# An attention-and-expert kernel on one core: a new order of all its operations, with some sixty of them on another engine

## The chip, the cores and the metric

The kernel runs on one core of a Trainium2 chip. The metric is device time in microseconds of one execution. The core has a matmul engine (TensorE, PE in the profile, with its weight loads as PEld), three engines for elementwise work (VectorE or DVE, ScalarE or ACT, GpSimd or POOL) and a queue for transfers between the chip's memory and the core (SyncE or SP). Each engine takes its instructions strictly in the order in which the program lists them; engines wait for each other through semaphores.

## The reference

A recurrent attention over 768 steps for 4 batches and 8 heads of size 48, then a feed-forward block in which the larger of two projections goes on:

```python
state = np.zeros((B, H, D, D))
for t in range(S):
    kt, vt, rt, wt = k[:, :, t], v[:, :, t], r[:, :, t], w[:, :, t]
    cur = np.einsum('bhd,bhe->bhde', u[None] * kt, vt)
    y[:, :, t] = np.einsum('bhd,bhde->bhe', rt, state + cur)
    state = wt[:, :, :, None] * state + np.einsum('bhd,bhe->bhde', kt, vt)
x = y.transpose(0, 2, 1, 3).reshape(B * S, H * D)      # 3072 x 384
out = np.maximum(x @ w1, x @ w2) @ w_out               # d_ff = 1024
```

All inputs and the output are float32.

## The kernel before

The recurrence is computed in chunks. A unit is one chunk of 256 steps of one or two batches; `UNITS` names eight: units 0 to 3 have one batch each and the first chunk, units 4 and 5 the second chunk and units 6 and 7 the third, with two batches each. For each unit the kernel loads w, k, r and v; takes logarithms of products of w and sums them over time on PE (`wp`, `ln`, `hi`, `lo`, `ex`); makes the sums' exponentials (`mz`, `ie`, `e0`); multiplies r and k by them (`rw`, `kw`, `scale`); transposes the results into the tile RK, on PE with an eviction (`tr`, `te`, units 0 to 4) or by DMA (`dt`, units 5 to 7); forms scores (`sc`), puts the masked ones into the tile M (`mk`), whose diagonal with u comes from `rk`, `ru`, `dg`, `dd` and `di`; computes the state (`kv`, `st`, `sm`, `sb`) and the output of the attention (`ya`, `yi`), which `xe` moves to xT. `vb` casts v to bf16.

The maximum is taken as max(a, b) = b + max(a - b, 0). So `wdiff` forms w1 - w2 in three pieces of 128 rows, `gt` multiplies xT by it, `rl` is the eviction with max(., 0), and `op` adds xT times the product w2 w_out (`wc`, made once by `w2turn`, `w2take`, `wocast`, `wfold`) and the rl result times w_out. `oe` evicts and `os` stores. `hot` are matmuls whose result nobody reads; 48 of them fill PE at fixed places in the order, eight or sixteen at a time.

A name like `scale.0.1.0.1@p` reads: the operation, the unit, its further arguments, and the engine (`@d` DVE, `@a` ACT, `@p` POOL); names without one have a fixed engine. For `scale` the arguments are 0 for r or 1 for k, the batch, and the half of the heads (units of two halves: unit 0 only). For `dt` they are r or k, and the batch.

What sets the order is one table, `ORDER`, of 652 such names. The program walks it once and issues each operation in that sequence, so it fixes the order on every engine and in the DMA queue, and the engine of each operation that may run on several. There is no scheduler beside it. On GpSimd operations of two full halves are issued as two pieces (`by_two`); on VectorE as one. Buffers are limited: four PSUM banks G for `ex`, `tr`, `w2turn`, `gt`, `op` and `hot`, two pairs Y for `sc`, `kv` and the attention's output. DMAs take eight semaphores in turn, so each is issued only when the one eight places before it has landed.

```python
for o in ORDER:
    o, _, e = o.partition("@")
    name, *a = o.split(".")
    a = [int(x) if x.isdigit() else x for x in a] + ([e] if e else [])
    if name in ops:
        ops[name](*a)
    else:
        unit[name](U[a[0]], *a[1:])
```

In the profile most elementwise products stand under line 176 (`mul`, one piece) or 180 (two pieces) and most copies and evictions under line 168 (`copy`), since helpers record them: the tile's name tells them apart. The other lines: 234 `hot`, 398 `ex` (395 and 396 from unit 3 on), 440 `mz`, 502 `dg`, 516 `di`, 565 `tr`, 596 `kv`, 615 `st`, 641 `sc`, 650 `mk`, 675 `yi`, 688 `ya`, 706 `gt`, 717 and 719 `rl`, 725 and 729 `op`, 743 `os`.

Of the kernel before, what the change touches and what calls it, by code (L numbers as in the profile page):

```python
# [53 lines left out]
zero.k.1@p zero.M.1@p load.1.w.0 zero.m@p mask zero.k.0@d load.0.w.0 u ident identb@p identq@a tri
wp.0.0@p ln.0.0 zero.s.0@d hot.8.3 zero.o@p load.0.k wp.1.0@d load.0.w.1 load.0.r wp.0.1@d hot.8.0
kw.0.1@p ln.0.1 ex.0.1 load.1.k ex.0.0 ln.1.0 wload.1.1 kw.0.0@p mz.0.0 ie.0.0 zero.v.1@d wt.0.0
uspread mz.0.1 ie.0.1 e0.0.1 zero.v.0@d wt.0.1 rw.0.1@d rk.0.0@d scale.0.0.0.1@d utake@a hot.8.2
we.0.0 load.1.r hot.8.1 rw.0.0@p ru.0.0@d zero.r@d e0.0.0 scale.0.0.0.0@d we.0.1 scale.0.1.0.1@p
scale.0.1.0.0@p ex.1.0 load.2.w.0 tr.0.0.0 zero.s.1@p te.0.0.0@a tr.0.0.1 te.0.0.1@a w2turn.1.0
load.0.v vb.0.0@a vb.0.1@p dg.0 load.1.v rk.1.0@d dd.0@a ru.1.0@d mz.1.0 sc.0.0.0.0 wload.1.2 kv.0  # L60
dg.1 ie.1.0 w2take.1.0@a sc.0.0.1.0 kw.1.0@p w2turn.2.0 load.3.w.0 wp.2.0@d vb.1.0@a st.0.0@a ln.2.0
di.0.0@d zero.M.0@p st.0.1 rw.1.0@d load.2.r wt.1.0 mk.0.0.0.0 sm.0@p w2take.2.0@a sc.0.0.1.1
sc.0.0.0.1 mk.0.0.0.1 mk.0.0.1.1 ex.2.0 we.1.0 e0.1.0 hot.8.5 vb.1.1@a dd.1@a zero.v.2@d sb.0.0@a
mz.2.0 scale.1.1.0.0@p scale.1.0.0.0@d ie.2.0 load.2.k rk.2.0@d w2turn.2.1 w2take.2.1@a tr.1.0.1
# [6 lines left out]
ru.2.0@d xe.1.0@a rl.0.2@a row.2 sm.1@d gt.1.1 load.3.r load.3.k rk.3.0@d gt.1.3 woload.2 mz.3.0
wocast.0@a rl.0.1@a ie.3.0 sc.2.0.1.0 woload.1 dg.2 dd.2@a rl.1.3@d kv.2 rl.1.1@d gt.0.3 st.2.0@a
rl.0.3@a woload.3 gt.1.0 st.2.1 gt.1.2 zero.M.2@p di.2.0@d e0.3.0 rw.3.0@p wocast.2@p load.3.v
sc.2.0.0.0 scale.3.0.0.0@d kw.3.0@p mk.2.0.0.0 gt.0.0 mk.2.0.1.0 ru.3.0@d wocast.1@p wocast.3@a
sb.2.0@a wfold.1 load.4.w.0 wp.4.0@d rl.1.0@a wfold.0 rl.1.2@a vb.3.1@d dg.3 wctake.0@a sb.2.1@a
scale.3.1.0.0@p wfold.2 ln.4.0 hi.4@d wctake.2@a dd.3@d ya.2.0.1.0 wctake.1@a di.3.0@d lo.4@d
rl.0.0@a row.3 ya.2.0.0.0 load.4.k load.4.r rk.4.0@d vb.3.0@p yi.2.0 kv.3 st.3.0@a st.3.1 xe.2.0@a
tr.3.0.0 te.3.0.0@a op.1.1 rk.4.1@d oe.1.1@a tr.3.0.1 te.3.0.1@a gt.2.0 gt.2.2 rl.2.2@a rw.4.0@d
gt.2.1 ru.4.1@p load.4.v wl.2 load.5.w.0 rl.2.1@a ex.4.0 mz.4.0 ex.4.1 wl.3 mz.4.1 row.4 rl.2.0@a
e0.4.1 sc.3.0.0.0 mk.3.0.0.0 sc.3.0.1.0 ie.4.0 gt.2.3 rl.2.3@a vb.4.1@a op.0.0 oe.0.0@a os.1.1  # L80
e0.4.0 sb.3.1@a vb.4.0@a op.0.1 sb.3.0@a scale.4.0.1.0@d oe.0.1@a mk.3.0.1.0 kw.4.0@p ru.4.0@d
ya.3.0.0.0 scale.4.1.1.0@d ya.3.0.1.0 scale.4.1.0.0@d yi.3.0 we.3 scale.4.0.0.0@d xe.3.0@a tr.4.1.1
tr.4.1.0 dg.4 sm.3@p load.5.k op.1.0 wp.5.0@p load.5.r te.4.1.0@a te.4.1.1@a ln.5.0 gt.3.2 oe.1.0@d
gt.3.0 sc.4.1.1.0 kv.4 hi.5@a tr.4.0.0 rl.3.0@a rl.3.2@a dd.4@d di.4.1@d tr.4.0.1 di.4.0@d lo.5@d
mk.4.1.1.0 gt.3.1 st.4.0 we.2 te.4.0.0@a sm.2@p st.4.1 rk.5.1@d load.6.w.0 op.2.1 te.4.0.1@a
rl.3.1@a rk.5.0@p ru.5.0@d oe.2.1@a sc.4.1.0.0 mk.4.1.0.0 sb.4.1@a load.5.v sc.4.0.1.0 gt.3.3
mk.4.0.1.0 ex.5.1 kw.5.0@p load.6.r ex.5.0 rl.3.3@a sb.4.0@a op.2.0 oe.2.0@a ya.4.1.0.0 ya.4.1.1.0
os.2.0 mz.5.0 mz.5.1 wl.4 rw.5.0@p row.5 sc.4.0.0.0 ru.5.1@p load.6.k op.3.0 e0.5.0 vb.5.1@a
mk.4.0.0.0 e0.5.1 ie.5.0 yi.4.1 xe.4.1@a oe.3.0@a scale.5.0.1.0@d yi.4.0 ya.4.0.1.0 ya.4.0.0.0
xe.4.0@a scale.5.0.0.0@d dt.5.0.0 op.3.1 wp.6.0@p ln.6.0 gt.4.6 dg.5 dd.5@a scale.5.1.0.0@d dt.5.1.0  # L90
rl.4.6@a gt.4.7 rl.4.7@a gt.4.0 we.4 rl.4.0@a gt.4.2 hi.6@d dt.5.0.1 gt.4.1 di.5.1@d oe.3.1@a
rl.4.2@a gt.4.4 vb.5.0@a scale.5.1.1.0@d sm.4@d lo.6@d gt.4.5 rk.6.1@d rl.4.4@a gt.4.3 rl.4.3@a
ex.6.0 rk.6.0@d kw.6.0@p rl.4.1@a kv.5 ru.6.0@p sc.5.0.1.0 di.5.0@d st.5.0 mk.5.0.1.0 st.5.1
rw.6.0@p rl.4.5@a op.4.2 ex.6.1 mz.6.1 sc.5.0.0.0 e0.6.1 dt.5.1.1 sc.5.1.0.0 os.1.0 mk.5.0.0.0
sb.5.0@a mk.5.1.0.0 op.4.3 load.7.w.0 mz.6.0 oe.4.3@a load.6.v e0.6.0 ya.5.0.0.0 ru.6.1@p oe.4.2@a
ya.5.0.1.0 ie.6.0 sc.5.1.1.0 mk.5.1.1.0 os.4.3 os.0.1 op.4.0 ya.5.1.0.0 sb.5.1@a ya.5.1.1.0 yi.5.1
load.7.k oe.4.0@a yi.5.0 op.4.1 dg.6 xe.5.1@a scale.6.0.1.0@d oe.4.1@a xe.5.0@d scale.6.0.0.0@d
dt.6.0.1 gt.5.1 wp.7.0@p scale.6.1.0.0@d ln.7.0 gt.5.3 rl.5.3@d gt.5.4 rl.5.4@a dd.6@d gt.5.6
vb.6.0@a gt.5.0 rl.5.0@a di.6.1@d rl.5.1@a hi.7@d di.6.0@d rl.5.6@a lo.7@d scale.6.1.1.0@p gt.5.7
rl.5.7@a vb.6.1@p kv.6 gt.5.2 rl.5.2@a load.7.r rk.7.0@d gt.5.5 ru.7.0@p dt.6.1.1 ex.7.1 mz.7.1  # L100
rl.5.5@a op.5.1 sc.6.1.0.0 rk.7.1@p dt.6.1.0 st.6.0 mk.6.1.0.0 ru.7.1@p dt.6.0.0 os.4.2 sc.6.1.1.0
mk.6.1.1.0 op.5.2 sb.6.0@a oe.5.2@a ex.7.0 mz.7.0 sc.6.0.1.0 wl.5 we.5 kw.7.0@p mk.6.0.1.0 os.3.1
sc.6.0.0.0 mk.6.0.0.0 op.5.3 os.3.0 ya.6.1.0.0 sb.6.1@a e0.7.1 rw.7.0@d ya.6.1.1.0 ie.7.0 os.4.1
e0.7.0 oe.5.3@a ya.6.0.1.0 scale.7.0.1.0@d ya.6.0.0.0 yi.6.0 yi.6.1 xe.6.0@a scale.7.0.0.0@d
oe.5.1@d op.5.0 xe.6.1@a gt.6.6 rl.6.6@a oe.5.0@a gt.6.2 load.7.v vb.7.0@a os.5.1 gt.6.5 rl.6.5@a
vb.7.1@a scale.7.1.0.0@p dt.7.1.0 gt.6.4 scale.7.1.1.0@p dg.7 dd.7@a dt.7.0.0 dt.7.0.1 rl.6.4@d
# [691 lines left out]
```

## Time and profile before

| | us |
|---|---|
| three runs | 151.09, 152.08, 153.25 |
| median of the runs | 152.08 |
| the profiled execution's own time | 149.86 |
| its span, first to last instruction | 148.2 |
| its mean granted TensorE clock | 0.977 of full |

Times in the tables that follow are microseconds from the start of the span. The profile's groups give the operation's busy time, the mean of one, and the idle time of the engine just before it with what ended it. A row of the timeline has the start, the length, the engine, the line, the operation with what it writes and reads, and how often; in brackets the idle time before it. An engine that idles costs nothing by itself: what counts is whether the work that the end waits for is held up.

### The profile page before, as it was taken

The numbers are of one execution on the slowest core, as the hardware profiler recorded it, in microseconds if no ns is written. First come the engines' busy times: TensorE is split into PE (matmuls) and PEld (weight loads), VectorE is DVE, ScalarE is ACT, GpSimd is POOL, SyncE is SP. The second block draws the span as 40 slices with busy tenths as digits, with TensorE's granted clock in tenths as the row PEclk, the third lists the DMA queues.
The fourth block names the chain that finished last, engine by engine and source line by source line (L and its number), as shares of the span: only waits on it lengthen the run. The fifth ranks groups of instructions, "written<-read, shape, count | busy, mean of one in ns | idle before, by whom it ended". The sixth has DMA issues, their size and how long they took to land.

```text
span 148.2 us, 5523 instructions
## 1 busy us (share of the span) xinstructions
PE 137.9 (93%) x2404; PEld 85.0 (57%) x2404; DVE 115.0 (78%) x160; ACT 93.7 (63%) x173; POOL 76.4 (52%) x94
## 2 busy tenths in 40 slices
...
GB/s 110 297 357 302 338 269 374 372 247 269 250 234 287 237 123 87 316 286 215 223 68 245 179 170 272 286 233 282 186 250 131 90 172 241 110 214 5 0 164 106
DMA packets 71188, 31.85 MB, mean 215 GB/s; under 512 B 66294, under 2 KB 70391, under 8 KB 71163
## 3 DMA queue, kind: packets, MB, share of 16 engines
...
q8 instruction: 19, 0.31, 0.9%
...
## 4 chain that ended last, share of the span: by engine, by line
PE 62%; DVE 13%; ACT 7%; DMA 5%; POOL 4%; issue 4%; SPq 2%; POOLq 1%; DVEq 0%; ACTq 0%
PE G L706 15%; PE G L729 15%; PE G L234 7%; PE G L725 6%; DVE M L650 5%; PE Y L688 4%; PE Y L641 3%; DMA lw<-in_w_dram 3%; PE G L318 3%; ACT RK L168 3%; DMA RK<-rp 2%; PE Y L675 2%; PE G L398 2%; POOL kp L180 2%; PE Y L596 1%
## 5 line engine op out<-in xcount | busy, mean ns | idle before, releaser
L729 PE MATMUL G<-wo_sb,gT 128*128 128x384 bf16 x192 | 35.1, 326 | 0.0
L706 PE MATMUL G<-xT,wd_sb 128*128 128x256 bf16 (+1 forms) x192 | 33.9, 326 | 0.1
L650 DVE CAST_PREDICATED M<-mask,Y 128x1024 bf16<-128x1024 int32 (+1 forms) x26 | 28.7, 1133 | 3.0 <-PE Y L641 2.9
L717 ACT ACTIVATE gT<-G 128x512 bf16<-128x512 f32 x41 | 23.4, 599 | 6.2 <-PE G L706 5.9
L729 PEld LDWEIGHTS <-gT 128*128 128x128 bf16 x192 | 18.8, 98 | 12.4
L706 PEld LDWEIGHTS <-wd_sb 128*128 128x128 bf16 x192 | 18.1, 98 | 12.5 <-issue 0.5
L180 POOL TENSOR_TENSOR rku<-rku,u_b 128x384 f32<-128x384 f32 x12 | 12.5, 1065 | 13.1 <-DVE rku L176 13.1
L234 PE MATMUL G<-S_b 128*128 128x512 bf16 x48 | 15.4, 488 | 2.1 <-DVE S_b L263 2.1
L725 PE MATMUL G<-wc_sb,xT 128*128 128x384 bf16 x72 | 15.7, 328 | 0.0
L168 ACT COPY RK<-G 128x1024 bf16<-128x1024 bf16 x12 | 11.8, 1016 | 6.0 <-PE G L565 6.0
L168 ACT COPY osb<-G 128x384 f32<-128x384 f32 x13 | 6.2, 477 | 12.7 <-PE G L729 10.8
L180 POOL TENSOR_TENSOR kp<-lk,iE 128x384 bf16<-128x384 f32 x10 | 11.2, 1147 | 1.8 <-issue 1.8
L234 PEld LDWEIGHTS <-S_b 128*128 128x128 bf16 x48 | 5.6, 123 | 11.0 <-issue 6.6
L168 ACT CAST xT<-Y 128x768 bf16<-128x768 f32 x10 | 10.2, 1033 | 2.4 <-PE Y L688 1.4
L502 DVE TENSOR_REDUCE dg<-rku 128x16 f32<-128x768 f32 x12 | 11.0, 944 | 0.0
L180 POOL TENSOR_TENSOR lk<-lk,lw 128x384 f32<-128x384 f32 x6 | 6.3, 1070 | 7.4 <-DVE rku L176 7.4
L641 PE MATMUL Y<-RK 48*64 48x128 bf16 x384 | 8.9, 220 | 1.2 <-ACT RK L168 0.5
L516 DVE TENSOR_TENSOR M<-identq,gd 128x512 int32<-128x512 int32 x12 | 9.0, 753 | 1.2 <-ACT gd L168 1.0
L440 DVE TENSOR_TENSOR MZ<-G,lg 128x384 f32<-128x384 f32 (+1 forms) x13 | 6.5, 513 | 3.6 <-PE G L398 2.1
L641 PEld LDWEIGHTS <-RK 48*64 48x64 bf16 x384 | 6.3, 106 | 4.9 <-issue 3.2
L688 PE MATMUL Y<-M,vp 64*32 64x128 bf16 x768 | 8.7, 219 | 0.3 <-DVE M L650 0.3
L176 DVE TENSOR_TENSOR rp<-lr,G 128x768 bf16<-128x768 f32 (+2 forms) x11 | 8.7, 795 | 0.4 <-ACT W L486 0.3
(108 smaller groups left out, 234.7 us busy)
## 6 DMA issues: line engine op xcount, KB each, us to landing
...
```

What stands on the lines that cost most here:

```text
L168: (nc.scalar.copy if e == "a" else nc.vector.tensor_copy if e == "d" else nc.gpsimd.tensor_copy)(o, i)
L180: op(o[:, g], a[:, g], b[:, g])
L234: nc.tensor.matmul(t, zz[:, 0:P], zz[:, 0:512], start=True, stop=True)
L502: nc.vector.reduce_sum(s.dg[:, b].rearrange("p i h -> p h i"), s.rku[:, b], axis=AX.X)
L516: (nc.vector if en == "d" else nc.gpsimd).tensor_tensor(out=o, in0=m, in1=g.unsqueeze(3).to_broadcast([P, 2, H, Q // 2]), op=ALU.bitwise_and)
L641: nc.tensor.matmul(t[q * Q:(q + 1) * Q, e, p * P:(p + 1) * P].rearrange("s (i g) -> s i g", i=2), s.kT[d, b, j, y * n + p, q, :], s.rT[d, ...
L650: nc.vector.copy_predicated(t[:, :, 2 * n * y:2 * n * (y + 1)].rearrange("s i (p e) g -> s p e i g", e=2), mask[:, j].bitcast(I32).unsquee ...
L688: nc.tensor.matmul(lhsT=s.vp[g, b, 2 * p + e, j, m * 32:(m + 1) * 32], rhs=s.M[b, j][g, :, 2 * p + e, :], **into(s, b, q, p * 96 + (e + m) ...
L706: nc.tensor.matmul(t[:, m * n * P:(m + 1) * n * P].rearrange("c (b t) -> c b t", t=P), wd_sb[:, ko, fo * P:(fo + 1) * P], s.xT[:, 0:n, ko, :],
L717: nc.scalar.activation(o, i, AF.Relu)
L725: nc.tensor.matmul(t[:, 0:HD], s.xT[:, a, ko, :], wc_sb[:, ko, :], start=(ko == 0), stop=False)
L729: nc.tensor.matmul(t[:, 0:HD], s.gT[:, c:c + P], wo_sb[:, f, :], start=False, stop=(f == FO - 1))
```

## The change

`ORDER` is written anew: the same 652 operations in another sequence, 66 of them on another engine. Nothing else in the program differs. Two lines of the table, as the diff has them, from the place where the differences of the weights stand:

```diff
-di.1.0@d mk.1.0.1.0 ln.3.0 wload.0.0 w2turn.0.1 w2take.0.1@a mk.1.0.0.0 trih@a vb.2.1@p ya.0.0.1.1
...
+woload.0 mk.1.0.1.0 wdiff.1@d tr.2.0.1 vb.2.0@a wdiff.0@d row.2 w2turn.1.0 load.3.r wdiff.2@d
```

Other engines: `wdiff.2`, `kw.0.0`, `rw.0.0`, `rw.3.0`, `wp.0.0`, `wp.5.0` to `wp.7.0`, `rk.5.0`, `ru.5.1`, `sm.3`, `sm.5` and `vb.3.0` go from GpSimd to VectorE; `rk.2.0`, `rk.5.1`, `rk.6.0`, `rk.7.0`, `kw.2.0`, `ru.3.0`, `ru.4.0`, `ru.5.0`, `scale.4.1.0.0`, `scale.5.1.0.0`, `scale.5.1.1.0` and `dd.3` from VectorE to GpSimd; `dd.0`, `dd.7`, `vb.1.0`, `vb.5.1` and `vb.6.0` from ScalarE to GpSimd, `wocast.1` the other way. Between VectorE and ScalarE casts of v, evictions (`oe`, `rl`, `xe`) and `hi` change in both directions, among them `vb.0.0`, `wocast.0`, `hi.3`, `rl.0.0` and `xe.3.0` to VectorE, `w2take.0.0`, `rl.1.1`, `hi.4` and `oe.1.0` to ScalarE.

On VectorE, around the forming of the weights' differences (the writes to wd_sb; M_81 is unit 1's scores, wb the turned w2, wst and lg the logarithms of unit 3). Before:

```order
L176 TENSOR_TENSOR rp_73<-lr,G 128x16x48
L615 TENSOR_TENSOR T<-Y,S_f 128x192
L516 TENSOR_TENSOR M_81<-identq,gd 128x2x256
L650 COPY_PREDICATED M_81<-mask,Y 128x8x2x64 x2
L168 CAST wb<-G 128x512
L176 TENSOR_TENSOR wd_sb<-gT 128x1024 x2
L413 SCALAR_TENSOR_TENSOR wst<-lg,wst 128x384
L176 TENSOR_TENSOR rku<-rku,u_b 128x768
```

Now:

```order
L176 TENSOR_TENSOR rp_73<-lr,G 128x16x48
L615 TENSOR_TENSOR T<-Y,S_f 128x192
L650 COPY_PREDICATED M_81<-mask,Y 128x8x2x64 x2
L176 TENSOR_TENSOR wd_sb<-gT 128x1024 x2
L176 TENSOR_TENSOR wd_sb<-wst 128x1024
L176 TENSOR_TENSOR rku<-rku,u_b 128x768
L168 CAST wo_sb<-wso 128x768
```

The third difference is now on VectorE, right behind the other two; the eviction to wb has left, and unit 1's diagonal (`di.1.0`) stands further up.

On GpSimd, in the head of the program, around the scaled keys of unit 0 (kp_74). Before:

```order
L176 TENSOR_TENSOR lw<-lk,lw 128x4x48 x2
L176 TENSOR_TENSOR lw<-lr,lw 128x4x48
L176 TENSOR_TENSOR kp_74<-lw,iE 128x4x48
L176 TENSOR_TENSOR kp_74<-lk,iE 128x4x48
L176 TENSOR_TENSOR kp_74<-lw,iE 128x4x48
L176 TENSOR_TENSOR kp_74<-lk,iE 128x4x48
L263 MEMSET S_b 128x1536
L168 CAST vp_76<-lv 128x4x2x48
L176 TENSOR_TENSOR lw<-lk,lw 128x8x48
```

Now:

```order
L186 AFFINE_SELECT mask<-mask 64x64 x2
L186 AFFINE_SELECT mask<-mask 64x128
L257 MEMSET M_81 128x1024
L176 TENSOR_TENSOR lw<-lk,lw 128x8x48
L176 TENSOR_TENSOR kp_74<-lw,iE 128x4x48
L176 TENSOR_TENSOR kp_74<-lk,iE 128x4x48
L176 TENSOR_TENSOR kp_74<-lw,iE 128x4x48
L176 TENSOR_TENSOR kp_74<-lk,iE 128x4x48
L168 CAST gd<-dg 128x32
L168 CAST vp_76<-lv 128x4x2x48
```

The mask, one clearing of M and the product for unit 1's keys (`kw.1.0`) now stand ahead of the scaled keys, the clearing of S_b stands at the program's start, and behind the keys comes the cast `dd.0` (gd).

In the DMA queue the loads of unit 0 now come first (half of w, r, k, u, the other half of w), then w of units 1 and 2; before, w of unit 1 came first. On PE the fillers at the start keep their sixteen matmuls; behind the first sums came sixteen more, and now eight come there and eight after unit 1's sums.

On GpSimd, where unit 5 is prepared (rku, lk, wso, kp_75; lg are the logarithms of later units, S_f the state). Before:

```order
L180 TENSOR_TENSOR rku<-wso,lk 128x384 x2
L180 TENSOR_TENSOR lk<-lk,wso 128x8x48 x2
L180 TENSOR_TENSOR wso<-wso 128x8x48 x2
L180 TENSOR_TENSOR rku<-rku,u_b 128x384 x2
L180 TENSOR_TENSOR lg<-lw 128x384 x2
L180 TENSOR_TENSOR lk<-lk,lw 128x8x48 x2
```

Now:

```order
L180 TENSOR_TENSOR rku<-rku,u_b 128x384 x2
L180 TENSOR_TENSOR rku<-wso,lk 128x384 x2
L180 TENSOR_TENSOR lk<-lk,wso 128x8x48 x2
L180 TENSOR_TENSOR wso<-wso 128x8x48 x2
L180 TENSOR_TENSOR kp_75<-lk,iE 128x8x48 x4
L168 CAST vp_76<-lv 128x8x2x48
```

Behind unit 5's four products now stand both its scaled keys (kp_75, four pieces) and a cast of v.

More of the change, by code (lines that the diff above doesn't have):

```diff
@@ L53 @@
 ORDER = """
[L54 to L64, printed above, removed]
@@ L71 @@
[L71 to L82, printed above, removed]
@@ L83 @@
[L83 to L106, printed above, removed]
@@ L113 @@
-oe.7.2@a op.7.0 os.7.2 oe.7.0@a os.6.1 os.7.0 op.7.3 oe.7.3@a os.7.3
+zero.o@p zero.s.0@d hot.8.1 load.0.w.0 ident hot.8.3 zero.s.1@p load.0.r wp.0.0@d ln.0.0 rw.0.0@d
+load.0.k u zero.r@d zero.M.2@p load.0.w.1 wp.0.1@d rw.0.1@d zero.v.0@d load.1.w.0 kw.0.0@d ln.0.1
+load.2.w.0 rk.0.0@d tri load.1.k ex.0.1 uspread utake@a ex.0.0 zero.m@p wp.1.0@d ln.1.0 identb@p
+mz.0.1 e0.0.1 ru.0.0@d wp.2.0@d mz.0.0 kw.0.1@p dg.0 mask zero.M.1@p hot.8.2 load.1.r rw.1.0@d
+kw.1.0@p wt.0.1 ex.1.0 ie.0.1 scale.0.1.0.1@p we.0.1 ie.0.0 scale.0.1.0.0@p dd.0@p zero.k.0@d wt.0.0
```

65 lines of the change are left out of this document (54 added, 11 removed).

## The prediction, made before the changed kernel had run

> **What bounds the kernel now.** I read the page's head first, then the table of busy time in three stretches of my own, then the timelines of the engines around the border of the first two. The head of the page:
>
> ```profile
> span 148.2 us, 5523 instructions
> PE 137.9 (93%) x2404; PEld 85.0 (57%) x2404; DVE 115.0 (78%) x160; ACT 93.7 (63%) x173; POOL 76.4 (52%) x94
> ```
>
> TensorE (PE) is busy in 93% of the span. Where the missing 10.3 us lie shows in the stretches: length, then busy time of PE, PEld, VectorE (DVE), ScalarE (ACT), GpSimd (POOL), clock, DMA share.
>
> ```profile
> 7.12:36.81 29.69, 26.30 (x413) 16.18 (x411) 24.22 (x44) 18.22 (x42) 19.82 (x21) 0.89 1.03 316
> 36.81:74.57 37.76, 36.89 (x704) 26.49 (x701) 36.76 (x50) 31.67 (x56) 20.83 (x21) 1.00 0.89 224
> 74.57:144.93 70.36, 69.61 (x1278) 40.49 (x1277) 52.54 (x66) 41.15 (x72) 30.18 (x31) 1.00 0.74 176
> ```
>
> From 36.81 on PE idles 37.76 - 36.89 = 0.87 us and 70.36 - 69.61 = 0.75 us: 1.6 us in 108. All orders issue the same matmuls, so hardly anything can be won there. In the first stretch PE looks busy too, but much of it is filler (the `hot` matmuls, whose result nobody reads). The timelines of PE and of DVE at the end of that stretch (start, length, engine, line, operation, count):
>
> ```profile
> 34.68 1.90 PE L234 MATMUL G<-S_b 128*128 128x512 bf16 x8
> 36.51 0.35 PE L675 MATMUL Y<-RK,S_b 128*32 128x128 bf16 x12
> 36.79 1.37 PE L706 MATMUL G<-xT,wd_sb 128*128 128x256 bf16 x11
> 34.46 2.35 DVE L176 TENSOR_TENSOR wd_sb<-gT 128x1024 bf16<-128x1024 f32 x2
> ```
>
> The first `gt` matmul (L706) starts at 36.79, when the second `wdiff` ends (34.46 + 2.35 = 36.81; ends are modelled). The 1.90 us of filler before it only covered this wait. So the time is: start of the `gt` phase, plus 108 us of dense PE work, plus an end (one eviction, one store) that is the same in both orders.
>
> What set that start, in the chain of waits:
>
> ```profile
> 2.81 4.29 DMA lw<-in_w_dram
> 7.12 0.37 DVE lg L176
> 11.42 5.16 PE G L234 x16
> ```
>
> The second half of unit 0's w lands at 7.10, `wp.0.1` follows at 7.12; DVE then works 24.22 of 29.69 us and waits 5.47. Nearly all these waits are five (DVE's timeline, the wait in brackets):
>
> ```profile
> 9.03 0.36 DVE L440 TENSOR_TENSOR MZ<-G,lg 128x192 f32<-128x192 f32 x1 [1.54 <-PE G L398]
> 17.26 0.56 DVE L440 TENSOR_TENSOR MZ<-G,lg 128x384 f32<-128x384 f32 x1 [0.56 <-PE G L398]
> 20.20 0.69 DVE L516 TENSOR_TENSOR M<-identq,gd 128x512 int32<-128x512 int32 x1 [1.05 <-ACT gd L168]
> 21.73 0.36 DVE L615 TENSOR_TENSOR T<-Y,S_f 128x192 f32<-128x192 f32 x1 [0.84 <-ACT S_f L168]
> 30.35 0.36 DVE L615 TENSOR_TENSOR T<-Y,S_f 128x192 f32<-128x192 f32 x1 [1.00 <-ACT S_f L168]
> ```
>
> **The change part by part.** *Loads.* Ahead of and with `load.0.w.1` stood 384 + 192 + 384 + 192 KB (w of unit 1, half w, k, half w); now 192 + 384 + 384 + 192 KB (half w, r, k, half w). The same 1152 KB, so I leave `wp.0.1` at 7.12. Term 0. The last `wload` had 8448 KB with and ahead of it, now 8064 KB (the first `woload` goes behind it): 8.26 MB at the first stretch's 316 GB/s are 26 us of transfer. That is ahead of the first `wdiff`, which by the sum below runs near 30.4, but not by much.
>
> *VectorE's work up to the last `wdiff`.* Prices by the groups that keep shapes apart (busy, mean ns):
>
> ```profile
> L176 DVE TENSOR_TENSOR wd_sb<-gT 128x1024 bf16<-128x1024 f32 x2 | 2.3, 1215 | 0.0
> L168 DVE CAST vp<-lv 128x384 bf16<-128x384 f32 x1 | 0.3, 345 | 0.0
> L176 DVE TENSOR_TENSOR rku<-lr,lk 128x768 f32<-128x768 f32 x9 | 8.5, 949 | 0.0
> L168 DVE CAST wb<-G 128x512 bf16<-128x512 f32 x1 | 0.7, 684 | 0.0
> ```
>
> Added: `wdiff.2` 1.215 (from POOL), `vb.0.0` 0.345 (from ACT), `kw.0.0` 0.37 (as `wp.0.1`), `wp.1.0`. Removed: `rk.2.0` 0.949 and `kw.2.0` (to POOL), `w2take.0.0` 0.684 (to ACT). `wp.1.0` and `kw.2.0` are the same product of 128x384 and cancel, so do `zero.k.0` and `zero.r`. Net +0.30: 24.22 + 0.30 = 24.52 us. Had DVE never to wait, `wdiff.2` would end at 7.12 + 24.52 = 31.64; with all the old waits, at 37.11. These are my bounds.
>
> *Which waits stay.* The 1.54 goes: `rw.0.1`, `zero.v.0`, `kw.0.0`, `rk.0.0` and `wp.1.0`, some 2.4 us of work, now lie between `wp.0.1` and the first `mz`. The 0.56 stays: `ex.1.0` has 8 fillers ahead of it instead of 16, but DVE comes earlier too. For the 1.05: `dd.0` goes from ACT (behind two evictions) to POOL, behind `scale.0.1.*`. POOL's rows:
>
> ```profile
> 1.26 0.95 POOL L257 MEMSET M<- 128x1024 bf16 x1
> 2.41 0.31 POOL L237 MEMSET mask<- 128x256 f32 x1
> 2.79 1.39 POOL L186 TENSOR_SCALAR_AFFINE_SELECT mask<-mask 64x64 f32<-64x64 f32 x6
> 10.42 1.27 POOL L176 TENSOR_TENSOR kp<-lw,iE 128x192 bf16<-128x192 f32 x1 [1.17 <-ACT iE L460]
> 11.65 0.59 POOL L176 TENSOR_TENSOR kp<-lk,iE 128x192 bf16<-128x192 f32 x1
> 15.85 1.71 POOL L176 TENSOR_TENSOR lw<-lk,lw 128x384 f32<-128x384 f32 x1
> ```
>
> Now `kw.0.1` (0.59, after `wp.0.1`: 7.5 to 8.1), mask and `zero.M.1` (2.65: 10.7), `kw.1.0` (up to 1.71: 12.5) and two pairs of 1.27 + 0.59 (16.2) stand ahead of `dd.0`; if nothing is slowed, the pairs take 4 x 0.59 and `kw.1.0` 1.0, and it is 14.1. DVE reaches `di.0.0` near 15.5, so it waits 0 to 0.9; I take 0.9, since the slow prices are of the very same operations. Of the two waits for `S_f` (1.84) I keep half, 0.94: `st.0.0` and `st.1.0` still stand on ACT behind evictions of RK, but DVE has the four `mk` of unit 0 between them. Kept: 0.56 + 0.9 + 0.94 = 2.40, so `wdiff.2` ends at 7.12 + 24.52 + 2.40 = 34.04 instead of 36.81. Here all three pieces must be done ahead of any `gt`, as before. Gain 2.75 us (bounds -0.3 and 5.2). POOL's old `wdiff.2` was long done and gave no wait; that VectorE takes it over costs its 1.2 us in full, and is in the sum.
>
> *What is late next.* ACT. Ahead of the first `rl` it now has `te.2.0.1`, `xe.1.0`, `w2take.0.0`, `xe.0.0`, `te.2.0.0` in a row:
>
> ```profile
> L168 ACT COPY RK<-G 128x1024 bf16<-128x1024 bf16 x12 | 11.8, 1016 | 6.0 <-PE G L565 6.0
> L168 ACT CAST xT<-Y 128x768 bf16<-128x768 f32 x10 | 10.2, 1033 | 2.4 <-PE Y L688 1.4 <-PE Y L675 1.0
> ```
>
> That is 2 x 1.02 + 2 x 1.03 + 0.6 = 4.7 us, while PE can run only until its four G banks are full. I put 0.4 us on it (between 0 and, if it all falls behind the start of `gt`, some 2.7, the whole gain).
>
> *The rest* (some 65 operations on another engine, orders of units 2 to 7): DVE gets about as much as it gives (in the second stretch `wocast.0`, `hi.3`, `rw.3.0`, `rl.0.0`, `wp.5.0`, `xe.3.0`, `rk.5.0` and four small ones against `rl.1.1`, `ru.3.0`, `ru.4.0`, `ru.5.0`, `rk.5.1`, `scale.4.1.0.0`, `hi.4`, `oe.1.0`: some 6 us each), POOL some 6 us more, priced as in the last rival (four `rk`, three `ru`, three `scale` against `wp.5` to `wp.7`, `rk.5.0`, `ru.5.1`, `wdiff.2`, `rw.3.0`, two `sm`). DVE waits 1.0 us in the second stretch, so both it and PE cover each other there; in the third it has 17.8 us to spare and POOL 40. Term 0, because PE's 108 us are the cover; its price if that fails is in the rivals.
>
> *Sum.* 2.75 - 0.4 = 2.3 us less than the profiled execution's 149.86, 147.5. The three runs stand at 151.09 to 153.25, all above it; the median is 2.2 us higher. I forecast for the median: 152.08 - 2.3 = **149.8 us**.
>
> **The rivals.** *More: the waits all go.* If the two bounds of POOL and ACT are met from below, the `gt` phase starts at 31.64 and nothing is given back: 152.08 - 5.1 = 147.0. For it: in the new order each consumer has other work ahead of it. Against: DVE has no order before with fewer than 5 us of waits.
>
> *No gain: VectorE is held by POOL.* The same product of 128x192 on POOL took 1.27 us while DVE ran `rk.0.0`, and 0.59 after it. DVE pays as well:
>
> ```profile
> L176 DVE TENSOR_TENSOR lr<-lr,lw 128x768 f32<-128x768 f32 x2 | 2.7, 1357 | 0.0
> ```
>
> against 949 for the same size in `rk`: 0.41 us. With six more pieces on POOL, 6 x 0.41 = 2.5 us on an engine that has 1.0 us to spare in the second stretch: the gain goes, 152.1. Against: the mean over all such products is far below 0.41. [...]
>
> *The half clock falls on real work.* One-microsecond windows, PE alone (busy, clock, DMA share, GB/s):
>
> ```profile
> 12.00:13.00 1.00, 1.00 (x5) 0.66 1.17 326
> 15.00:16.00 1.00, 1.00 (x5) 0.63 1.08 358
> 22.00:23.00 1.00, 0.90 (x18) 0.78 0.95 371
> 25.00:26.00 1.00, 1.00 (x4) 0.51 1.08 323
> ```
>
> Between the first pair and between the second the clock is 0.50: from about 12.3 to 15.7 and 22.6 to 26.0, 3.4 us each. Both mostly hit fillers (16 took 5.16 us; at full clock 8 took 1.90). If such a window falls on `gt` or `op`, it costs 3.4 / 2 = 1.7 us; two of them, 149.8 + 3.4 = 153.2. [...]
>
> *Slower: unit 5's keys come late.* `scale.5.1.*` and `vb.5.1` now queue on POOL behind `ru.5.0`, `rk.5.1`, `kw.5.0`, `rw.5.0`, and PE's `kv.5` needs them all:
>
> ```profile
> 67.84 1.96 POOL L180 TENSOR_TENSOR rku<-wso,lk 128x384 f32<-128x384 f32 x2
> 69.88 3.29 POOL L180 TENSOR_TENSOR lk<-lk,wso 128x384 f32<-128x384 f32 x2
> 98.20 0.85 POOL L168 CAST vp<-lv 128x768 bf16<-128x768 f32 x1
> 111.90 4.63 POOL L180 TENSOR_TENSOR kp<-lk,iE 128x384 bf16<-128x384 f32 x4
> 85.74 0.80 PE L596 MATMUL Y<-vp,kp 64*64 64x48 bf16 x64
> ```
>
> 3 x 1.96 + 3.29 + 4.63 + 0.85 = 14.7 us after `rk.5.0`. PE comes to `kv.5` at 85.74 - 2.3 - 1.6 (two `gt` and an `ex` go behind it) = 81.8, so it decides from an `rk.5.0` that ends at 67.1; each us later is one us more. Ending at 72.5 it gives 149.8 + 5.4 = 155.2. Against: by the new order it runs ahead of `di.4.1`, some 2 us ahead of that point or more.
>
> **How the numbers follow.** About 2% (3.0 us) is what a measurement of this kernel can tell from no change. Forecast (gain 1 to 3.1 us, 149.0 to 151.1) 0.38; waits all go (147.0 to 149.0) 0.30; held by POOL (151.1 to 152.5) 0.16; half clock on real work (151.5 to 153.2) 0.06; late keys (155 and more) 0.10. Range 147.2 to 152.8: it leaves out the late keys, the end of the clock's case and the lowest bound, under 2 in 10. Faster by over 2% is below 149.04: 0.30 + 0.02 of the forecast's edge = 0.32; slower (above 155.1) 0.10; within, 0.58.
>
> **What would show it.** The first L706 near 34 us, `wdiff` three in a row on DVE and ending with it; DVE's waits between 7 and 34 us about 2.4 us; PE idle after the start of `gt` near 2 us. Wrong, if the second half of w lands later than 7.5, if L706 starts before 32.5 or after 36, or if PE waits more than 3 us after it, at `kv.5` (L596) or behind an `rl`.

## The result: 1.3% slower, with the gain at the start lost in stalls of TensorE

| | before | after |
|---|---|---|
| median of twenty runs each, us | 150.37 | 151.73 |
| lowest to highest, us | 148.40 to 153.25 | 149.94 to 155.23 |
| ratio after to before, 95% interval | | 1.0128 (1.0088 to 1.0168) |
| profiled execution, us | 149.86 | 152.06 |
| first `gt` matmul, us from the start | 36.79 | 35.24 |

The forecast was a gain of 2.3 us. The ratio is that of each kernel's faster runs, while the medians are over all twenty. The profiled execution after, first the head of its page, with TensorE's busy tenths and granted clock in 40 slices:

```profile
span 150.3 us, 5532 instructions
PE 136.7 (91%) x2402; PEld 84.5 (56%) x2404; DVE 116.4 (77%) x166; ACT 90.4 (60%) x164; POOL 88.9 (59%) x101
...
PE   5899797969999999999959999399999999999991
...
PEclk9999959999999999999999999959999999999999
```

Behind the start the row of PE has two holes, the 5 and the 3, where before it had none of that kind; and the clock, which dips to 5 once in the head, does so again at some 98 us. The stretches up to the last `wdiff`, then the `gt` phase in two parts (columns as in the prediction):

```profile
6.93:33.70 26.77, 22.47 (x396) 14.86 (x398) 24.27 (x46) 16.95 (x38) 20.85 (x29) 0.94 1.07 326
35.24:72.92 37.68, 37.68 (x667) 26.94 (x663) 36.35 (x50) 32.46 (x60) 26.59 (x25) 1.00 0.93 239
72.92:147.05 74.13, 69.85 (x1317) 39.84 (x1315) 52.56 (x66) 37.34 (x63) 37.38 (x34) 0.98 0.68 157
```

The first 38 us of the phase are without a gap. In the last 74.13 us PE idles 4.28. The sum against before: the phase starts 1.55 us earlier; PE idles 4.28 us in it instead of 1.62 (+2.66); it is busy 107.53 us instead of 106.52, counted from the first `gt` at 36.79 (+1.01). That makes 2.1, the difference of the spans (150.3 and 148.2). The waits of PE for its matmuls to Y, in total us, times, longest:

```profile
PE Y L688 <- issue: 5.5, 3, 2.4
```

"Issue" means that the engine waited for nothing the profile shows. PE's timeline at the three places, in units 0/1, 4 and 5 (start, length, line, count; the wait in brackets):

```profile
30.80 0.36 PE L688 MATMUL Y<-M,vp 64*32 64x128 bf16 x19
32.40 0.73 PE L688 MATMUL Y<-M,vp 64*32 64x128 bf16 x61 [1.24 <-issue]
33.06 1.90 PE L234 MATMUL G<-S_b 128*128 128x512 bf16 x7
...
35.24 2.02 PE L706 MATMUL G<-xT,wd_sb 128*128 128x256 bf16 x17
...
73.11 0.86 PE L675 MATMUL Y<-RK,S_b 128*32 128x128 bf16 x48
73.91 1.13 PE L688 MATMUL Y<-M,vp 64*32 64x128 bf16 x107
76.89 0.35 PE L688 MATMUL Y<-M,vp 64*32 64x128 bf16 x21 [1.85 <-issue]
...
93.09 0.53 PE L675 MATMUL Y<-RK,S_b 128*32 128x128 bf16 x24
93.55 1.23 PE L688 MATMUL Y<-M,vp 64*32 64x128 bf16 x115
97.16 0.30 PE L688 MATMUL Y<-M,vp 64*32 64x128 bf16 x13 [2.38 <-issue]
97.40 1.14 PE L725 MATMUL G<-wc_sb,xT 128*128 128x384 bf16 x3
98.33 2.67 PE L729 MATMUL G<-wo_sb,gT 128*128 128x384 bf16 x8
```

Each stall stands inside a group of equal small matmuls whose operands were there for the ones ahead of it. The same work of unit 4 in the kernel before:

```profile
73.72 0.75 PE L688 MATMUL Y<-M,vp 64*32 64x128 bf16 x64
74.63 0.42 PE L641 MATMUL Y<-RK 48*64 48x128 bf16 x16 [0.16 <-DVE M L650]
74.98 0.66 PE L725 MATMUL G<-wc_sb,xT 128*128 128x384 bf16 x3
75.48 1.46 PE L729 MATMUL G<-wo_sb,gT 128*128 128x384 bf16 x8
76.87 0.86 PE L675 MATMUL Y<-RK,S_b 128*32 128x128 bf16 x48
77.67 0.75 PE L688 MATMUL Y<-M,vp 64*32 64x128 bf16 x64
```

Before, `sc` and one `op` stood in the middle; the new order has all 176 `yi` and `ya` of unit 4 in one run. What the places have in common appears only when PE's instructions are counted in the order of the trace: matmuls, weight loads, and the few that only wait or handle semaphores (16 in all in the changed kernel, 7 to 9 of them ahead of these places). PE stands ahead of numbers 704, 2496 and 3264, in the kernel before (0.65 and 0.37 us) ahead of 960 and 3264, give or take two. Each is 192 plus a multiple of 256. So it is with all 42 waits of PE of over 0.3 us for "issue", behind the first 5 us, in the fourteen traces of this document. And the page's DMA queues have one that moves 19 packets of 16 KB in all:

```profile
q8 instruction: 19, 0.31, 0.9%
```

PE has 4822 recorded instructions, and the numbers 192, 448 and so on up to 4800 are 19 as well: one packet for each border. So a packet is read here as a block of 256 instructions; by the 16 KB that is 64 bytes for each, an estimate. For each place, the border one block ahead of the stall, the packet that follows it, and PE's return, from the trace:

| units | border crossed | packet starts | takes | PE goes on | after the packet's start |
|---|---|---|---|---|---|
| 0/1 | 27.13 | 29.87 | 1.04 | 32.40 | 2.53 |
| 4 | 73.46 | 74.49 | 0.95 | 76.89 | 2.40 |
| 5 | 93.22 | 94.58 | 1.16 | 97.16 | 2.58 |

Theory A: PE's instructions come in blocks of 256; a packet starts some time after PE has crossed a border (0.4 to 4.9 us for 33 of the 38 packets in the two traces; the other five, all in the last 35 us, start when PE still has 9 to 39 instructions to go to it, which is not explained), and the next border can be passed only about 2.5 us after the packet's start. A block that runs faster than that ends in a stall. A block of `ya` alone takes about 1.4 us; in the kernel before, the blocks of the same places, with an `op` among them, took 3.6 and 3.85 us.

Theories B, C and D were the rivals: a wait for data that the profile doesn't show, an artefact of profiling, and costs of the moves between VectorE and GpSimd.

### The profile page after: what moved, and what is told of

The parts are those of the page before. It is cut to its first block, busy times and chain, and to the rows that moved or that the text cites. A ratio compares the mean times of both kernels' runs of the same rounds, so it can differ in the third digit from the quotient of the medians.

```text
span 150.3 us, 5532 instructions
## 1 busy us (share of the span) xinstructions
PE 136.7 (91%) x2402; PEld 84.5 (56%) x2404; DVE 116.4 (77%) x166; ACT 90.4 (60%) x164; POOL 88.9 (59%) x101
## 5 line engine op out<-in xcount | busy, mean ns | idle before, releaser
L729 PE MATMUL G<-wo_sb,gT 128*128 128x384 bf16 x192 | 36.5, 334 | 0.1
L180 POOL TENSOR_TENSOR rku<-rku,u_b 128x384 f32<-128x384 f32 x16 | 21.3, 1352 | 21.2 <-DVE rku L176 21.2
L180 POOL TENSOR_TENSOR kp<-lk,iE 128x384 bf16<-128x384 f32 x16 | 17.5, 1117 | 0.5 <-POOL lr L180 0.5
L234 PE MATMUL G<-S_b 128*128 128x512 bf16 x46 | 13.6, 444 | 2.1 <-DVE S_b L263 1.8
L168 ACT CAST xT<-Y 128x768 bf16<-128x768 f32 x9 | 9.1, 1025 | 9.3 <-PE Y L688 5.0
L180 POOL TENSOR_TENSOR rku<-lr,lk 128x384 f32<-128x384 f32 x8 | 9.8, 1243 | 3.9 <-issue 3.9
L688 PEld LDWEIGHTS <-vp 64*32 64x32 bf16 x768 | 7.1, 90 | 7.6 <-issue 7.3
L516 DVE TENSOR_TENSOR M<-identq,gd 128x512 int32<-128x512 int32 x12 | 10.3, 868 | 1.2 <-POOL gd L168 1.2
L719 DVE TENSOR_SCALAR gT<-G 128x512 bf16<-128x512 f32 x8 | 5.4, 682 | 5.8 <-PE G L706 5.8
L168 ACT COPY wb<-G 128x384 f32<-128x384 f32 x7 | 3.4, 481 | 9.3 <-PE G L729 9.3
```

Of the source, the lines that this page charges most:

```text
L168: (nc.scalar.copy if e == "a" else nc.vector.tensor_copy if e == "d" else nc.gpsimd.tensor_copy)(o, i)
L180: op(o[:, g], a[:, g], b[:, g])
L234: nc.tensor.matmul(t, zz[:, 0:P], zz[:, 0:512], start=True, stop=True)
L516: (nc.vector if en == "d" else nc.gpsimd).tensor_tensor(out=o, in0=m, in1=g.unsqueeze(3).to_broadcast([P, 2, H, Q // 2]), op=ALU.bitwise_and)
L688: nc.tensor.matmul(lhsT=s.vp[g, b, 2 * p + e, j, m * 32:(m + 1) * 32], rhs=s.M[b, j][g, :, 2 * p + e, :], **into(s, b, q, p * 96 + (e + m) ...
L729: nc.tensor.matmul(t[:, 0:HD], s.gT[:, c:c + P], wo_sb[:, f, :], start=False, stop=(f == FO - 1))
```

## Experiments

A group of fillers cut into narrower matmuls adds PE instructions without adding work. With `SPLIT` the program differs from the changed kernel only here:

```diff
-    def hot(n, _):
+    def hot(n, x):
...
-        for _ in range(n):
-            nc.tensor.matmul(t, zz[:, 0:P], zz[:, 0:512], start=True, stop=True)
+        m = SPLIT.get(x, 1)
+        for _ in range(n * m):
+            nc.tensor.matmul(t[:, 0:512 // m], zz[:, 0:P], zz[:, 0:512 // m], start=True, stop=True)
```

**112 more instructions, new order.** `SPLIT = {1: 3, 3: 3, 2: 2, 0: 2, 5: 2}`.

> The new order, nothing moved; five of its filler groups ahead of the ya of units 0 and 1 are cut into two or three narrower matmuls each (the same columns in sum, 510 or 512 for one of 512), so PE has 112 more instructions (56 matmuls, 56 weight loads) ahead of all that follows. Theory A (PE's instructions come in blocks of 256 by the DMA queue that the profile names instruction, and PE stands where a block is run in less time than the fetch of the next one needs): the stalls of 1.24, 1.85 and 2.38 us at L688 in units 0/1, 4 and 5 go, since the block borders now lie so that each block there holds 3.5 us of work or more; one new stall of 1.5 to 2.5 us comes in unit 6's ya and yi (near 110 us, a block of 1.4 us), none of the others over 0.5. In sum some 3 to 4 us less than the changed kernel: 147.5 to 149, ratio to the kernel before 0.98 to 0.99. Theory B (PE waits there for data or a semaphore that the profile does not show): the stalls stay at the same places, 1.01. Theory C (the stalls are an artefact of profiling): they move in the trace, the timed ratio stays 1.01. Theory D (the loss is from the moves between VectorE and GpSimd): 1.01.

Measured: 147.09 us, ratio 0.986 (0.976 to 0.996). Its waits, unit 4's run and unit 6's run (lines stand two further down):

```profile
PE Y L677 <- issue: 1.6, 1, 1.6
PE G L567 <- issue: 1.6, 1, 1.6
```

```profile
72.71 0.86 PE L677 MATMUL Y<-RK,S_b 128*32 128x128 bf16 x48
73.50 1.30 PE L690 MATMUL Y<-M,vp 64*32 64x128 bf16 x128
...
109.00 0.51 PE L677 MATMUL Y<-RK,S_b 128*32 128x128 bf16 x18
111.13 0.63 PE L677 MATMUL Y<-RK,S_b 128*32 128x128 bf16 x30 [1.62 <-issue]
```

The same 176 matmuls of unit 4, in the same sequence, now run without a gap; the stalls of units 0/1, 4 and 5 are gone, and unit 6, which had none, has one. One more of 1.60 us came at 34.55 in unit 2's transposes (L567), where the expectation had at most 0.5. B, C and D fall as main causes: nothing else moved (the 68 operations, not 66, that the two tables give to another engine stay there), and the timed runs follow. The profiled span is 4.6 us shorter than the changed kernel's: 0.4 by an earlier `gt` (34.84), 2.6 by less idle time of PE behind it (1.67 instead of 4.28) and 1.5 by less busy time, since no stretch at half the clock falls there.

**160 more instructions, the kernel before.** The same edit of `hot`, `SPLIT = {1: 3, 3: 3, 2: 3, 0: 3, 5: 3}`.

> The kernel before, nothing moved; five filler groups are cut into three narrower matmuls each, so PE has 160 more instructions ahead of unit 0's ya. Theory A: stalls appear that the kernel before does not have, behind L675 or L688 in unit 0/1's run (a block of 1.6 us), in unit 6's (2.3 us) and in unit 7's (1.3 us), of 0.5 to 2 us each, 3 to 4 us in sum, some of the first covered by the wait for the last wdiff; the 0.65 at L596 and 0.37 at L675 go. Time 152.5 to 154, ratio 1.015 to 1.025. Theories B, C and D: no new stall, or none that the timed runs show; ratio 1.00 within 0.003.

Measured: 156.1 us, ratio 1.031 (1.017 to 1.044). PE's timeline at the three places named:

```profile
35.43 0.29 PE L690 MATMUL Y<-M,vp 64*32 64x128 bf16 x10 [2.09 <-issue]
...
115.19 0.24 PE L690 MATMUL Y<-M,vp 64*32 64x128 bf16 x6 [2.41 <-issue]
...
136.83 0.30 PE L690 MATMUL Y<-M,vp 64*32 64x128 bf16 x11 [2.39 <-issue]
```

A kernel whose order nobody touched loses 3% by where its block borders fall. The loss is more than the forecast 3 to 4 us. Its profiled execution had a granted clock of 0.967, but the loss is there at the same clock too: the three runs at 0.977 to 0.978 average 154.1 us, against 150.7 for the 31 of the kernel before at 0.973 to 0.977.

**256 more instructions, new order: the control.** `SPLIT = {1: 4, 3: 4, 2: 4, 0: 4, 5: 5}`.

> The control of the cut fillers: the new order with its five filler groups cut into four or five narrower matmuls each, 256 more instructions on PE ahead of units 0 and 1, a whole block. Theory A: the block borders fall on the same instructions again as in the changed kernel, so its three stalls are back at the same places (L688 of units 0/1, 4 and 5, some 1.2, 1.9 and 2.4 us, each within 1 us), ratio to the kernel before 1.005 to 1.02. The rival to A here (narrower fillers, which change the clock or the power at the start, help by themselves): as with 112 more, 0.98 to 0.99 and no stall in units 4 and 5.

Measured: 153.53 us, ratio 1.026 (1.020 to 1.033).

```profile
33.36 0.73 PE L690 MATMUL Y<-M,vp 64*32 64x128 bf16 x61 [1.79 <-issue]
...
78.76 0.35 PE L690 MATMUL Y<-M,vp 64*32 64x128 bf16 x21 [2.76 <-issue]
...
99.20 0.30 PE L690 MATMUL Y<-M,vp 64*32 64x128 bf16 x13 [2.54 <-issue]
```

The counts 61, 21 and 13 are those of the changed kernel: the stalls are back at the same instructions. The page of this run counts 20 packets of instructions instead of 19, one more for 256 more. Cutting the fillers does not help by itself; that narrower ones change the clock or the power was a supposition that no run here shows. Each stall is longer than in the changed kernel, and the ratio lies above the forecast; at a granted clock of 0.986 to 0.989 its four runs average 153.1 us and the changed kernel's seven (0.989) 152.8.

**The kernel before with its runs joined.** In units 4 and 5, `op` and `sc` go ahead of the `ya` instead of between them:

```diff
-op.2.0 oe.2.0@a ya.4.1.0.0 ya.4.1.1.0 ... sc.4.0.0.0 ... op.3.0
+op.2.0 oe.2.0@a op.3.0 sc.4.0.0.0 ya.4.1.0.0 ya.4.1.1.0 ...
-ya.5.0.0.0 ... ya.5.0.1.0 ... sc.5.1.1.0 ... op.4.0 ya.5.1.0.0
+op.4.0 sc.5.1.1.0 ya.5.0.0.0 ... ya.5.0.1.0 ... ya.5.1.0.0
```

> The kernel before with four pieces moved and nothing else: in units 4 and 5, op.3.0 and sc.4.0.0.0, and op.4.0 and sc.5.1.1.0, go from the middle of the ya and yi to ahead of them, so that the small matmuls stand in one run of 176, as the change has them. Theory A: the block borders 2240 to 2496 and 3008 to 3264 (counted in PE's instructions) then lie wholly within the two runs, 1.4 us of work each instead of 3.6 to 3.9; a stall of 1.5 to 2.8 us comes in each, with some 22 ya left in unit 4's run and some 13 yi in unit 5's. 3 to 5 us slower than before: ratio 1.02 to 1.03. Theories B and D: the same work in an order that asks no more of any other engine, 1.00 within 0.005, or a wait for M that the profile names.

Measured: 156.41 us, ratio 1.036 (1.021 to 1.051). PE's timeline (lines stand three further up):

```profile
77.92 0.35 PE L685 MATMUL Y<-M,vp 64*32 64x128 bf16 x21 [1.18 <-issue]
...
95.46 0.74 PE L685 MATMUL Y<-M,vp 64*32 64x128 bf16 x64 [0.65 <-DVE M L647]
...
99.21 0.61 PE L672 MATMUL Y<-RK,S_b 128*32 128x128 bf16 x13 [2.34 <-issue]
```

Both stalls come, 21 `ya` and 13 `yi` before the end of the runs, as counted beforehand, the first shorter than forecast. Not all of the loss is theirs: `op.4.0` no longer covers the masks, and PE waits 0.65 us for M. A third stall, of 1.03 us, comes at 33.60 in units 0/1, where nothing was moved: there the packet started 2.57 us after its border, in the kernel before 0.62. It costs nothing that shows, since `gt` starts at 36.35, 0.4 us earlier than before.

**The runs broken, new order.** `op.3.0` and `op.4.0` go into the middle of the runs of units 4 and 5:

```diff
-vb.5.0@a op.3.0 os.0.0 yi.4.0 ... ya.4.0.1.0 ya.4.0.0.0
+vb.5.0@a os.0.0 yi.4.0 ... ya.4.0.1.0 op.3.0 ya.4.0.0.0
-load.7.k op.4.0 yi.5.1 ... ya.5.0.0.0 dt.6.0.1
+load.7.k yi.5.1 ... ya.5.0.0.0 op.4.0 dt.6.0.1
```

> The new order with two pieces moved and nothing else: op.3.0 from ahead of unit 4's yi and ya into their middle, op.4.0 from ahead of unit 5's into theirs, so that 1.3 us of long matmuls lie within each run of small ones. Theory A: each of the two stalls shrinks by about the 1.3 us of the op that is now within the block: 1.85 to 0.5 to 0.9, 2.38 to 1.1; the 1.24 in units 0/1 stays. Some 2 us less than the changed kernel, ratio to the kernel before 0.995 to 1.005. Theory B: the stalls keep their length wherever the op stands, if what they wait for is the runs' own data; 1.01. Theory D: 1.01.

Measured: 151.18 us, ratio 1.012 (1.004 to 1.020): the forecast gain didn't come. The waits say why:

```profile
PE Y L686 <- issue: 4.0, 3, 1.8
PE Y L673 <- DVE M L648: 2.1, 2, 1.3
```

The stalls did shrink, in unit 5 from 2.38 to 0.83 and in unit 4 from 1.85 to 1.43, while that of units 0/1 was 1.76 this time. But `op.3.0` and `op.4.0` had stood where they hid the masks; without them PE waits for VectorE, 0.79 us in unit 4 and 1.33 in unit 5. Here a long matmul could cover only one of the two.

**`wdiff.2` back on GpSimd, new order.** `wdiff.2@d` becomes `wdiff.2@p`, nothing else.

> The new order with wdiff.2 back on GpSimd, where the kernel before had it. [...] Theory A: the start of the gt phase is set by PE's own stall in units 0/1 and the fillers behind it, not by the last wdiff; no change beyond 0.5 us, ratio 1.01.

Measured: 154.83 us, ratio 1.039 (1.028 to 1.050), so the expected "no change beyond 0.5 us" did not hold. GpSimd, VectorE, ScalarE and PE in the trace:

```profile
29.20 4.40 POOL L178 TENSOR_TENSOR wd_sb<-wst 128x512 bf16<-128x512 f32 x2 [0.96 <-DMA wst<-in_moe_w_dram]
33.56 1.71 POOL L174 TENSOR_TENSOR lg<-lw 128x384 f32<-128x384 f32 x1
...
32.40 2.02 DVE L174 TENSOR_TENSOR rku<-rku,u_b 128x768 f32<-128x768 f32 x1
...
35.30 0.52 ACT L385 ACTIVATE lg<-lg 128x384 f32<-128x384 f32 x1 [5.65 <-POOL lg L174]
...
37.69 5.10 PE L704 MATMUL G<-xT,wd_sb 128*128 128x256 bf16 x30 [3.53 <-ACT xT L166]
```

`wdiff.2` starts when its rows of the weights have landed and holds GpSimd for 4.40 us; `wp.3.0` queues behind it, ScalarE's `ln.3.0` waits 5.65 us for that, and the evictions to xT queue behind `ln.3.0`, so `gt` starts 2.45 us later than in the changed kernel. So in this order the move of `wdiff.2` to VectorE was needed, and D, by which the time should have come down with that move taken back, falls for this part. VectorE's product with u_b (rku, at 32.40) took 2.02 us beside the second piece of `wdiff.2`, of some 2.2 us, and `wp.3.0`, against 0.95 for the same one in the run with 112 more instructions. The traces show these 1.07 us, not what they come from.

**Less traffic at unit 5's packet.** `load.7.k` moves behind unit 5's run:

```diff
-scale.6.1.1.0@p load.7.k op.4.0
+scale.6.1.1.0@p op.4.0
-xe.5.1@a ln.7.0
+xe.5.1@a load.7.k ln.7.0
```

> The new order with load.7.k (768 KB) moved from ahead of unit 5's run to behind it, nothing else. Theory A has two parts here. A1 (the fetch of the next block is asked for when a border is crossed and waits in the busy data queues; it began 1.36 us after the border at unit 5): with less traffic the fetch begins some 0.5 us after the border and the stall of 2.38 us there falls to 1.3 to 1.7; units 0/1 and 4 keep theirs; ratio to the kernel before 1.005. A2 (the delay does not come from the loads): the stall stays within 0.3 us of 2.38, ratio 1.012.

Measured: 151.31 us, ratio 1.002 (0.993 to 1.011).

```profile
77.31 0.51 PE L688 MATMUL Y<-M,vp 64*32 64x128 bf16 x21 [2.96 <-issue]
...
97.99 0.30 PE L688 MATMUL Y<-M,vp 64*32 64x128 bf16 x13 [1.16 <-issue]
```

Unit 5's stall falls from 2.38 to 1.16, by more than the first expectation had; its packet started 0.4 us after the border instead of 1.36. But unit 4's went from 1.85 to 2.96 with nothing moved near it. So the packet's delay differs between executions, and one execution can't settle how much of it the loads make. It speaks for it that unit 5's packet started 1.4 to 2.0 us after the border in all four profiles of the new order with the load in its place and the borders here (its stall was 2.38, 2.54 and 2.65 where the run was left whole); against it, that unit 4's delay ranged from 1.0 to 2.3 us in the same profiles and this one.

**A better version.** 96 more instructions (`SPLIT = {1: 3, 3: 2, 2: 2, 0: 2, 5: 2}`) alone, and with one `op` inside unit 6's run:

```diff
-e0.7.0 op.5.1 op.5.3 mz.7.1 ... ya.6.1.1.0 ya.6.0.0.0 ... ya.6.1.0.0 ... ya.6.0.1.0 ... yi.6.1 xe.6.1@a
+e0.7.0 op.5.1 mz.7.1 ... ya.6.1.1.0 ... ya.6.1.0.0 ... yi.6.1 op.5.3 ya.6.0.0.0 ya.6.0.1.0 ... xe.6.1@a
```

> The new order with 96 more instructions instead of 112. Theory A: as with 112 (no stall in units 0/1, 4 and 5, one of 1.3 to 2 us in unit 6's run), but the block that ended in unit 2's transposes (1.60 us of stall at 34.55) now holds over 4 us of work, so that stall goes too and gt starts at 33.2 to 33.8 instead of 34.84; a block at unit 2/3's kv and yi holds 3.2 us and may stall by up to 0.5. 1 to 1.5 us less than with 112: 145.5 to 147, ratio 0.97 to 0.98.

> As with 96 more instructions, and op.5.3 (1.3 us of long matmuls) is moved from ahead of unit 6's run of small matmuls into it, between the half of unit 6 that is ready first and the other. Theory A: the block there holds 2.7 instead of 1.4 us and its stall shrinks from some 1.6 to about 0.3; if the masks of the second half come late without op.5.3 ahead, up to 0.5 us of it is given back as a wait for M. 0.8 to 1.3 us less than with 96 alone: 144.5 to 146, ratio 0.96 to 0.97, faster than both kernels.

Measured: alone 149.25 us, ratio 0.989 (0.981 to 0.997); with `op.5.3` 147.18 us, 0.982 (0.974 to 0.989). Both gained less than forecast. Alone it was not faster than 112: `gt` started at 33.58 as expected, but a stall of 0.99 us came right behind, one of 1.03 at 49.95, two smaller ones of 0.54 and 0.39, and unit 6's was 2.27. With `op.5.3` in the run, unit 6's was 1.15 and PE waited for no mask there. The second version was measured again beside one with 80 (`SPLIT = {1: 2, 3: 2, 2: 2, 0: 2, 5: 2}`):

> As the best so far (96 more instructions, op.5.3 within unit 6's run), with 80 more instead of 96. Theory A: blocks that took 3.2 us at 49.8 (stall 0.77) and that ended in gt at 35.2 (stall 0.99) now hold 0.3 to 0.5 us more, so some 0.5 to 1 us of stalls goes; unit 6's stays near 1. Ratio to the kernel before 0.975 to 0.98.

> The kernel with 96 more instructions and op.5.3 within unit 6's run once more, beside the one with 80. If its first measurement (0.982) was no accident of that chip's day: 0.975 to 0.988, and its profile again has no stall of over 0.6 us in the runs of units 4 and 5 and about 1 us in unit 6's.

> The kernel with 80 more instructions once more, since its one profile was taken at a granted clock of 0.76 throughout. Theory A alone: stalls of at most 2.5 us in sum after the start of gt, as with 96, and a time within 0.5% of that one. If it is again 1% or more slower than the one with 96 while the profile shows no more stalls, something other than the block borders sets that difference.

With 80: 149.39 us, ratio 0.997 (0.992 to 1.001), and again 148.91 us, 0.990 (0.973 to 1.007). With 96 again: 147.99 us, 0.989 (0.981 to 0.996). Its profile the second time:

```profile
36.25 3.12 PE L708 MATMUL G<-xT,wd_sb 128*128 128x256 bf16 x27 [1.47 <-issue]
...
112.08 0.52 PE L677 MATMUL Y<-RK,S_b 128*32 128x128 bf16 x22 [0.41 <-issue]
```

Both intervals of 96 with `op.5.3` lie below 1, so it beats both kernels, by 1 to 2% against the one before. But much of that goes with the granted clock. A stretch of 3.41 us at half the clock, as the two traces of the kernel before and the changed one have it, takes 0.011 off the mean clock of a span of 150 us; so by this estimate runs at 0.996 and above hold no whole one. Their means (from several chips):

| | runs at 0.996 and above | mean, us |
|---|---|---|
| kernel before, beside the experiments | 3 of 67 | 147.8 |
| changed kernel | 9 of 20 | 150.5 |
| 112 more | 5 of 6 | 146.7 |
| 96 more | 3 of 6 | 147.7 |
| 96 more and `op.5.3`, twice | 6 of 6, 11 of 12 | 147.2, 148.0 |

At the same clock the changed kernel loses 2.7 us, and the versions with cut fillers gain 1.1 us or next to nothing; the rest of the 1 to 2% goes with the clock: by the estimate above, 25 of their 30 runs have no whole stretch at half of it, and the kernel before has one or more in 64 of 67 (0.989 or less). What brings that difference was not tried. The forecast that 80 would be better by another 0.5 us missed. In its second profile there were stalls of 1.15, 0.85, 0.32 and 1.54 us and a wait of 1.09 us for a transpose (the first was taken at a clock of 0.76 throughout and can't be compared), against 1.47 and 0.41 with 96. The length of a block alone does not give these: the packets' delays differ too.

## Why the prediction was wrong, step by step

- *Loads, term 0.* Right: `wp.0.1` at 6.93 (forecast 7.12).
- *VectorE up to the last `wdiff`.* Right in the sum. Busy 24.27 us of 26.77, so 2.50 of waits (forecast 24.52 and 2.40), the end at 33.70 (34.04). The waits are partly others: that for gd came, 1.18 instead of 0.9; those for `S_f` went, and one of 1.04 for unit 2's exponentials came.

```profile
16.98 0.95 DVE L516 TENSOR_TENSOR M<-identq,gd 128x512 int32<-128x512 int32 x1 [1.18 <-POOL gd L168]
...
26.82 0.95 DVE L176 TENSOR_TENSOR rp<-lr,G 128x768 bf16<-128x768 f32 x1 [1.04 <-ACT G L436]
```

- *`gt` starts with the last `wdiff`.* Wrong by 1.5 us: 35.24, not 33.70. PE itself came late, 1.24 of it by the stall, and the filler and eight transposes stood between. With 96 more instructions `gt` started at 33.6 to 34.3. I had taken PE in the first stretch for an engine that only waits.
- *ACT gives back 0.4.* It gave back nothing: after the start of `gt` PE has no wait for an eviction in the list of waits.
- *"Term 0, because PE's 108 us are the cover."* This step failed. It asked of the other engines whether they would keep up, and they did. It did not ask whether PE's own instructions would: moving `op` out of the middle of `ya` and `yi` changes none of PE's work, and cost 1.85 + 2.38 us against 0.65 + 0.37 before. The text named "PE waits more than 3 us after it" as the sign of an error, and 4.28 us it was, though not at the places it watched. The sentence "All orders issue the same matmuls, so hardly anything can be won there" has the same gap: much could be lost there.
- *The rivals.* Unit 5's late keys did not come: there is no wait at `kv.5`. VectorE held by GpSimd: by its own terms, 2.5 us less the 1.0 to spare, it makes 151.3 us and not 152.1; a VectorE product that takes longer, 2.02 us instead of 0.95, is seen in the run with `wdiff.2` on GpSimd, where it stands beside a chain through ScalarE. That GpSimd holds VectorE was not shown, and in the changed kernel no wait of PE behind the start of `gt` is for VectorE. The half clock on real work did come in the profiled execution. Windows of one microsecond (PE busy, clock):

```profile
97.00:98.00 1.00, 0.84 (x15) 0.41 (x16) 0.16 (x1) 0.47 (x1) 1.00 (x2) 0.68 0.56 125
98.00:99.00 1.00, 1.00 (x5) 0.47 (x4) 0.00 (x0) 1.00 (x2) 1.00 (x3) 0.50 1.29 266
99.00:100.00 1.00, 1.00 (x5) 0.48 (x4) 0.00 (x0) 0.97 (x2) 0.55 (x1) 0.50 0.13 23
100.00:101.00 1.00, 1.00 (x5) 0.47 (x4) 0.00 (x0) 0.12 (x1) 0.00 (x0) 0.61 0.04 4
```

  From some 97.4 to 100.8 the clock is 0.50: eight matmuls of `op.4.1` took 2.67 us instead of 1.46. That is one window, 1.7 us at most (PE's busy time in the phase grew by 1.0), right behind the stall of 2.38. The other traces point to the stalls: leaving out the one at 0.76, seven such windows of 3.41 us begin later than 27 us, and each begins from 0.2 us before to 1.4 us after the end of a stop of PE of 2.27 us or more, six of them a stall and one the wait of 3.53 for xT. But four stops of 2.29 to 2.76 us had none behind them, so what decides is open. And the forecast took the two windows of the kernel before as mostly harmless, on fillers: its runs at 0.973 to 0.977 average 150.7 us, against 147.8 at 0.996 and above.
- *What stands when the borders lie well.* The new order with 112 or 96 more instructions came to 0.986 and 0.989 of the kernel before; the forecast, 149.8 of 152.08, was 0.985. That agreement is partly luck: at the same granted clock the gain is 1.1 us or less, not 2.3, and these versions still stall, at other places.
- *The number.* The measured median, 151.73 us, lies within the stated range of 147.2 to 152.8, but that is luck too: the forecast stood on the median of three runs, 152.08, and that of twenty is 150.37. From there the same gain would have given 148.1.

What stays open: what sets the delay between border and packet, why some packets start ahead of their border, why PE goes on only some 1.4 us after a packet of 1.0 us has landed, and which stalls have a stretch at half the clock behind them.
